# A schedule change in a fused retention + ELU-MLP kernel: attention one unit further ahead, late ELU pass, hand-made plan for units 4 to 11

## Chip, cores, metric

One core of a Trainium2 chip. The metric is the device time of a run in microseconds (us), the median of several runs. "Span" is the time from the first to the last instruction in one profiled run. The "granted clock" is the share of TensorE's full clock that its throttle let through.

## The reference

```python
def _attn_ref(q, k, v):                     # each [8 batches, 8 heads, 576, 64]
    scores = (1 / np.sqrt(64)) * np.matmul(q, k.transpose(0, 1, 3, 2))
    gamma = 1.0 - 2.0 ** (-5.0 - np.arange(H))
    Dmat = np.where(rel >= 0, gamma[:, None, None] ** rel, 0.0)
    return np.matmul(scores * Dmat, v)

def _moe_ref(x, w_in, w_out):               # x [4608, 512], w_in [512, 2048], w_out [2048, 512]
    h = x @ w_in
    g = np.where(h > 0.0, h, np.exp(np.minimum(h, 0.0)) - 1.0)
    return g @ w_out
```

The kernel cuts the 4608 tokens into 36 units of 128 (unit 0 to 35). The units form ten groups: group 0 is units 0 to 3, group 1 is 4 and 5, group 2 is 6 and 7, groups 3 to 9 have four units each. FFN1 of a group needs the attention output `xt` of all its units.

## The kernel before

Names used below. `rqk`, `rv`: a unit's raw q, k, v. `qkn`, `vn`: their bf16 forms. `tr`: transposes in PSUM, copied to `qkT`. `sc`: scores. `pt`: masked scores. `o`: attention product. `ph`: FFN1 output in PSUM, three banks plus one lent by `pm`. `e`, `m`, `g`: the ELU chain on ScalarE (ACT), GpSimd (POOL) and VectorE (DVE). A "slot" is one FFN1 tile or a quarter of an FFN2 row block: four matmuls of 512 columns, or eight of 256.

```python
ps_h = ctx.enter_context(tc.tile_pool(name="ps_h", bufs=3, space=PSUM))   # ph
ps_m = ...bufs=1   # pm          ps_s = ...bufs=1   # sc
ps_o = ...bufs=1   # o           ps_st = ...bufs=1  # st

def turn(u, bank=None):                     # transposes of unit u
    ...
    if u < PE_TURNED:                       # 12
        pool, tag = bank or (ps_o, "o")
        ps = pool.tile([P, 2, HP, P], BF16, name="tr", tag=tag)
        ... 8 TensorE transposes ...
        nc.vector.tensor_copy(t[:, 0], ps[:, 0]); nc.scalar.copy(t[:, 1], ps[:, 1])
    else:
        nc.sync.dma_start_transpose(...)    # by DMA

def stretch(u, ahead=True):
    if ahead: scores(u + 1)
    inter(u); state(u); intra(u)            # the product, into o
    if ahead: masks(u + 1)                  # pt
    put_x(u); state_out(u)                  # xt

def ffn1(g, ft, bank=None):
    ... matmuls into ph ...
    nc.scalar.activation(e, ph, AF.Exp)
    nc.gpsimd.tensor_scalar(m, e, -1.0, 1.0, ALU.add, ALU.mult)
    nc.vector.scalar_tensor_tensor(gt_, ph, 0.0, m, ALU.max, ALU.min)     # g, at once

def prep(u, *engs):                         # casts q and k, scales v; u >= 12: turn by DMA
    ...

for ft in range(NFT):                       # FFN1 of group 0
    ffn1(0, ft, ...)
    if ft == 5:
        load(4, nc.vector)                  # a 1-element memset on VectorE holds the loads back
        for u in range(5, 12): load(u)
for u in range(4): ffn2_half(u, 0)          # needs w_out pieces 0 and 1
prep(4, A, V)
ffn2_half(0, 1)                             # needs w_out pieces 2 and 3
turn(4)
... units 4 to 11 between ffn2_half, FFN1 of groups 1 and 2, FFN2 of group 1 (cut) ...
for g in range(2, NG + 1):                  # FFN1 of g and FFN2 of g - 1 in turns
    ...
    at[-1] -= 3                             # last unit of group g + 1: three slots before the end
```

## Time and profile before

| | before |
|---|---|
| median, 4 runs | 346.38 us (344.27 to 346.76) |
| span of the profiled run | 344.1 us, granted clock 0.994 |
| TensorE busy | 313.9 us |
| start of FFN1 of group 0, transposes of unit 4, FFN1 of group 3, FFN1 of group 4 | 22.7, 47.7, 106.4, 133.0 us |

The last row cuts the run into stages, each read from the timeline of TensorE. The prediction below shows the lines of the profile.

### The profile page before, as it was taken

The page shows a single profiled execution, that of the slowest core. Times are in us where ns is not written, and L with a number is a line of the kernel's source. Part 1 is how long each engine was busy: PE and PEld are TensorE (multiplying, and loading weights), DVE is VectorE, ACT ScalarE, POOL GpSimd, SP SyncE. Part 2 cuts the span into 40 slices and gives each one's busy share as a digit, 9 for nine tenths or more (in the row PEclk, how much of TensorE's full clock was granted, in tenths as well). Part 3 has the DMA queues.
Part 4 walks back from the last instruction along what each step waited for, and adds up shares of the span by engine and source line. Part 5 has one row for each costly group of instructions (what it writes and reads, how often), then busy time and mean ns, then how long its engine had stood idle before and what let it go on. Part 6 is the DMA issues. An engine that isn't in the chain of part 4 may idle for free.

```text
span 344.1 us, 7077 instructions
## 1 busy us (share of the span) xinstructions
PE 313.9 (91%) x2797; PEld 163.0 (47%) x2797; DVE 193.8 (56%) x290; ACT 134.1 (39%) x241; POOL 137.2 (40%) x205
## 2 busy tenths in 40 slices
PE   8889988669488999999899989989998999999995
PEld 3544676555354544445344535444444444444442
DVE  3637534575746787666566746684667465444400
ACT  6436322453233543434344334333343443344411
POOL 3587312353423554444344534443444423233300
PEclk9999999999989999999999999999999999999999
DMA  9999999995069689679857777769878120000021
GB/s 171 198 156 201 184 262 240 225 209 90 4 156 209 150 165 231 134 149 192 179 135 168 158 154 153 154 150 158 168 171 155 60 65 32 30 32 30 30 92 62
DMA packets 149922, 48.70 MB, mean 142 GB/s; under 512 B 138625, under 2 KB 145793, under 8 KB 149889
## 3 DMA queue, kind: packets, MB, share of 16 engines
q1 hardware_dynamic: 141888, 41.96, 59.6%
q0 software_dynamic: 6272, 4.19, 8.5%
q10 hardware_dynamic: 1728, 2.10, 1.9%
q8 instruction: 22, 0.36, 0.5%
q14 instruction: 12, 0.09, 0.1%
HBM read 36.70 MB, written 9.44 MB: 134 GB/s over the span
## 4 chain that ended last, share of the span: by engine, by line
issue 31%; PE 22%; POOL 20%; DVE 12%; SPq 6%; DMA 6%; ACT 1%; POOLq 0%; DVEq 0%; ACTq 0%
POOL m L314 13%; PE pm L329 12%; PE ph L307 9%; SPq L85 6%; POOL vn L177 5%; DVE pt L215 4%; DVE qkn L168 3%; DMA rv<-in_v_dram 3%; DVE g L316 3%; DMA rqk<-in_k_dram 3%; DVE xt L279 2%; POOL w_out_sb L100 1%; POOL w_in_sb L95 1%; PE sc L206 0%; PE o L266 0%
## 5 line engine op out<-in xcount | busy, mean ns | idle before, releaser
L316 DVE SCALAR_TENSOR_TENSOR g<-ph,m 128x512 bf16<-128x512 f32 x144 | 98.4, 688 | 106.6 <-POOL m L314 106.6
L314 POOL TENSOR_SCALAR m<-e 128x512 bf16<-128x512 f32 x144 | 89.6, 624 | 164.1 <-ACT e L312 161.6
L307 PE MATMUL ph<-xt,w_in_sb 128*128 128x512 bf16 (+1 forms) x640 | 145.4, 359 | 6.2 <-DVE xt L279 5.9
L312 ACT ACTIVATE e<-ph 128x512 f32<-128x512 f32 x144 | 85.9, 597 | 141.1 <-PE ph L307 138.9
L329 PE MATMUL pm<-w_out_sb,g 128*128 128x512 bf16 x512 | 129.7, 381 | 1.4 <-DVE g L316 0.7
L307 PEld LDWEIGHTS <-w_in_sb 128*128 128x128 bf16 x640 | 60.3, 98 | 68.1 <-issue 9.2
L329 PEld LDWEIGHTS <-g 128*128 128x128 bf16 x512 | 49.7, 98 | 60.3 <-issue 2.4
L215 DVE TENSOR_TENSOR pt<-sc,mask 128x1024 bf16<-128x1024 f32 x36 | 43.7, 1214 | 6.1 <-PE sc L206 6.0
L177 POOL TENSOR_TENSOR vn<-rv,gk 128x512 bf16<-128x512 f32 x36 | 38.1, 1059 | 17.7 <-DMA rv<-in_v_dram 17.7
L279 DVE TENSOR_TENSOR xt<-o,gx 128x512 bf16<-128x512 f32 x36 | 24.4, 678 | 1.1 <-PE o L266 1.1
L168 DVE CAST qkn<-rqk 128x1024 bf16<-128x1024 f32 x26 | 24.2, 932 | 0.0
L339 ACT COPY ot<-pm 128x512 f32<-128x512 f32 x31 | 18.1, 585 | 15.4 <-PE pm L329 15.4
L206 PE MATMUL sc<-qkT 64*64 64x128 bf16 x576 | 15.0, 222 | 4.4 <-ACT qkT L192 2.7
L206 PEld LDWEIGHTS <-qkT 64*64 64x64 bf16 x576 | 9.4, 106 | 18.8 <-issue 10.3
L266 PE MATMUL o<-pt,vn 128*64 128x128 bf16 x288 | 14.5, 222 | 2.4 <-DVE pt L215 2.4
L190 PE MATMUL tr<-ident,qkn 128*128 128x128 bf16 x96 | 7.9, 226 | 9.6 <-DVE xt L279 7.8
L258 ACT CAST sb<-st 128x256 bf16<-128x256 f32 x32 | 11.9, 372 | 10.7 <-PE st L249 7.7
L192 ACT COPY qkT<-tr 128x512 bf16<-128x512 bf16 x12 | 7.0, 585 | 22.7 <-DVE qkT L191 22.7
L348 PE MATMUL pmh<-w_out_sb,g 128*128 128x256 bf16 x128 | 15.0, 273 | 0.6 <-DVE g L316 0.5
L362 PE MATMUL dum<-warm 128*128 128x512 bf16 x45 | 13.8, 440 | 1.3 <-DVE warm L108 1.3
L348 PEld LDWEIGHTS <-g 128*128 128x128 bf16 x128 | 12.3, 98 | 2.7 <-DVE g L316 0.8
L232 PE MATMUL o<-qkT,sb 64*64 64x128 bf16 (+1 forms) x256 | 12.3, 214 | 0.4 <-DVE xt L279 0.4
(43 smaller groups left out, 84.1 us busy)
## 6 DMA issues: line engine op xcount, KB each, us to landing
rqk<-in_q_dram SPq DMA_DIRECT2D x32, 256.0 KB, 4.1
rqk<-in_k_dram SPq DMA_DIRECT2D x32, 256.0 KB, 4.8
rv<-in_v_dram SPq DMA_DIRECT2D x32, 256.0 KB, 5.0
out_dram<-ot SPq DMA_DIRECT2D x28, 256.0 KB, 2.0
w_in_sb<-in_moe_w_in_dram POOLq DMA_DIRECT2D x4, 512.0 KB, 7.1
w_out_sb<-in_moe_w_out_dram POOLq DMA_DIRECT2D x4, 512.0 KB, 16.0
rqk<-in_q_dram SPq DMA_DIRECT2D x8, 128.0 KB, 4.4
rqk<-in_k_dram SPq DMA_DIRECT2D x8, 128.0 KB, 4.4
```

The costliest lines, as they stand in the source:

```text
L85: nc.sync.dma_start(dst, src[b, :, s0 : s0 + n, :].rearrange("h p d -> p h d"))
L168: engs[0](n, src)
L177: nc.gpsimd.tensor_tensor(n, rv, gk[:, u % R].unsqueeze(2).to_broadcast([P, H, D]), ALU.mult)
L206: nc.tensor.matmul(sc[j * 64 : (j + 1) * 64, i, hp], t[r, 1, hp, j * 64 : (j + 1) * 64], t[r, 0, hp], start=(hp == 0), stop=(hp == HP - 1) ...
L215: nc.vector.tensor_tensor(pt.rearrange("p i h t -> p (i h) t"), scs[u].rearrange("p i h t -> p (i h) t"), m.unsqueeze(1).to_broadcast([P, ...
L279: nc.vector.tensor_tensor(xts[g][:, :, i * P : (i + 1) * P], os_[u], gx[:, :, s0 : s0 + P], ALU.mult)
L307: nc.tensor.matmul(ph[:, i * n : (i + 1) * n], w_in_sb[:, j, f : f + P], xts[g][:, j, :n], start=(j == 0), stop=(j == KJ - 1), skip_group_ ...
L312: nc.scalar.activation(e, ph, AF.Exp)
L314: nc.gpsimd.tensor_scalar(m, e, -1.0, 1.0, ALU.add, ALU.mult)
L316: nc.vector.scalar_tensor_tensor(gt_, ph, 0.0, m, ALU.max, ALU.min)
L329: nc.tensor.matmul(pm, gts[g, ft][:, it * P : (it + 1) * P], w_out_sb[:, ft], start=(ft == 0), stop=(ft == NFT - 1))
L348: nc.tensor.matmul(pm, gts[g, ft][:, it * P : (it + 1) * P], w_out_sb[:, ft, c * 256 : c * 256 + 256], start=(ft == 0), stop=(ft == NFT - 1),)
```

## The change

Its intent is to keep TensorE busy from unit 4 on: no transposes behind `xt`, no FFN1 that waits for the last unit of its group, and no cast, `pt` or `xt` behind a `g` that still waits for its `m`.

```diff
-            pool, tag = bank or (ps_o, "o")
+            pool, tag = bank or (ps_s, "sc")
...
+    def finish(n=0):
+        while late and late[0][0] <= slot[0] - n:
+            _, gt_, ph, m, _ = late.pop(0)
+            nc.vector.scalar_tensor_tensor(gt_, ph, 0.0, m, ALU.max, ALU.min)
+    def tick():                             # called at the end of each ffn1 and ffn2
+        slot[0] += 1
+        finish(3)
...                                         # in ffn1
-        nc.vector.scalar_tensor_tensor(gt_, ph, 0.0, m, ALU.max, ALU.min)
+        late.append((slot[0], gt_, ph, m, (g, ft)))
...                                         # unit 2 of the start
-                G(seen, raws[3][0][0:1, 0, 0, 0:1])      # waits for Q of unit 3
+                G(seen, raws[3][0][0:1, 1, 0, 0:1])      # waits for K of unit 3
                 load_w_in(0)
+                load_w_in(1)
...
-    prep(4, A, V)
+    prep(4, A, G)                           # K cast on POOL, for units 4 to 11
...
+    plan = [(1, 1, n) for n in range(8)] + [(2, 1, n) for n in range(3)]
+    for n in range(5):
+        plan += [(1, 2, n), (2, 1, n + 3)]
+    plan += [(1, 2, n) for n in range(5, 8)]
+    at = {6: (1, 4), 7: (6, 8), 8: (10, 12), 9: (14, 16), 10: (18, 19), 11: (21, 23)}
+    for n, (what, g, s) in enumerate(plan):
+        (f1 if what == 1 else ffn2)(g, s)
+        for u, (a, b) in at.items():
+            if n == a:
+                scores(u); masks(u)
+                prep(u + 1, A, G) if u < 11 else None
+            if n == b:
+                product(u)
+                if u < 11: turn(u + 1)
+                if u > 8: prep(u + 3, V)
+                load_next()
+    scores(12); masks(12)
...                                         # groups 3 and later
-        at[-1] -= 3
+            if n in (4, 9, 13, 18, 23) if g == 3 else n % 8 == 7:
+                ... prep, load_next, stretch of the next unit: five units in group 3's stage
```

More of the change, by code (lines that the diff above doesn't have):

```diff
@@ L297 @@
     gts = {}
+    slot = [0]
+    late = []
+    def finish(n=0):
[5 more added lines that the diff above has]
+        finish(3)
     def ffn1(g, ft, bank=None):
@@ L315, in ffn1 @@
         gt_ = gpool.tile([P, 512], BF16, name="g", tag="g")
-        nc.vector.scalar_tensor_tensor(gt_, ph, 0.0, m, ALU.max, ALU.min)
+        late.append((slot[0], gt_, ph, m, (g, ft)))
         for i in range(512 // n):
             gts[g, ft + i] = gt_[:, i * n : (i + 1) * n]
+        tick()
     acc = {}
@@ L323, in ffn2 @@
         it, part = divmod(s, 4)
+        if late and (g, part * 4 + 3) >= late[0][4]:
+            finish()
         if part == 0:
@@ L331, in ffn2 @@
             )
+        tick()
         if part == 3:
@@ L377, in load_next, with product @@
             nload[0] += 1
+    def product(u):
+        inter(u)
+        state(u)
+        intra(u)
+        put_x(u)
+        state_out(u)
     seen = const.tile([1, 1], FP32, name="seen")
@@ L389 @@
         inter(u)
-        state(u)
-        masks(u)
         if u < 3:
+            state(u)
+            masks(u)
             if u == 2:
-                G(seen, raws[3][0][0:1, 0, 0, 0:1])
+                G(seen, raws[3][0][0:1, 1, 0, 0:1])
                 load_w_in(0)
+                load_w_in(1)
             cast(u + 1, A, A if u == 2 else G)
@@ L400 @@
         else:
+            masks(u)
             dummy(4)
+            state(u)
         intra(u)
@@ L405 @@
         dummy(2)
-    for n in range(1, 4):
+    for n in range(2, 4):
         load_w_in(n)
@@ L415 @@
                 load(u)
+    finish()
     for u in range(4):
         ffn2_half(u, 0)
-    prep(4, A, V)
+    prep(4, A, G)
     ffn2_half(0, 1)
     turn(4)
-    prep(5, A, V)
     ffn2_half(1, 1)
+    prep(5, A, G)
     scores(4)
-    inter(4)
-    state(4)
     masks(4)
     ffn2_half(2, 1)
-    intra(4)
-    put_x(4)
-    state_out(4)
+    product(4)
     turn(5)
@@ L433 @@
     scores(5)
-    prep(6, A, V)
-    inter(5)
-    state(5)
     masks(5)
-    dummy(4)
-    intra(5)
-    put_x(5)
-    state_out(5)
+    prep(6, A, G)
+    dummy(5)
+    product(5)
     turn(6)
-    for i in range(8):
-        ffn1(1, 2 * i, (ps_m, "pm") if i % 4 == 3 else None)
-        if i == 0:
-            prep(7, A, V)
-            scores(6)
-            masks(6)
-        if i == 1:
-            inter(6)
-            state(6)
-            intra(6)
-            put_x(6)
-            state_out(6)
-        if i == 2:
-            turn(7)
-        if i == 4:
-            scores(7)
-            masks(7)
-            prep(8, A, V)
-        if i == 6:
-            stretch(7, ahead=False)
-            prep(9, A, V)
-            load_next()
@@ L465, with f1 @@
-    turn(8)
-    for g in range(2, NG + 1):
-        f1 = [(0, g, s) for s in range(0, NFT, 4 // len(GROUPS[g]))] if g < NG else []
-        f2 = [(1, g - 1, s) for s in range(4 * len(GROUPS[g - 1]))]
-        tot = len(f1) + len(f2)
-        seq = []
+    def f1(g, n):
+        ffn1(g, 2 * n, (ps_m, "pm") if g == 1 and n == 3 else None)
+    plan = [(1, 1, n) for n in range(8)] + [(2, 1, n) for n in range(3)]
+    for n in range(5):
+        plan += [(1, 2, n), (2, 1, n + 3)]
+    plan += [(1, 2, n) for n in range(5, 8)]
@@ new lines @@
+    at = {6: (1, 4), 7: (6, 8), 8: (10, 12), 9: (14, 16), 10: (18, 19), 11: (21, 23)}
[3 more added lines that the diff above has]
+            if n == a:
+                scores(u)
+                masks(u)
+                prep(u + 1, A, G) if u < 11 else None
+            if n == b:
+                product(u)
+                if u < 11:
+                    turn(u + 1)
+                if u > 8:
+                    prep(u + 3, V)
+                load_next()
@@ L472 @@
+    scores(12)
+    masks(12)
+    nxt = [12]
+    for g in range(3, NG + 1):
+        f1s = [(ffn1, g, s) for s in range(NFT)] if g < NG else []
+        f2s = [(ffn2, g - 1, s) for s in range(4 * len(GROUPS[g - 1]))]
+        tot = len(f1s) + len(f2s)
         a = b = 0
         for n in range(tot):
-            if b * len(f1) < a * len(f2) and b < len(f2) or a >= len(f1):
-                seq.append(f2[b])
+            if b * len(f1s) < a * len(f2s) and b < len(f2s) or a >= len(f1s):
+                f, gg, s = f2s[b]
@@ L476 @@
                 b += 1
             else:
-                seq.append(f1[a])
+                f, gg, s = f1s[a]
                 a += 1
-        if g == 2:
-            seq = f2[:2] + [x for ab in zip(f1, f2[2:] + [None, None]) for x in ab if x]
-        nxt = list(GROUPS[g + 1]) if g + 1 < NG else []
-        at = [n for n, (what, gg, s) in enumerate(seq) if what and s % 4 == 3]
-        if g == 3:
-            at = [len(seq) * (i + 1) // 4 - 1 for i in range(4)]
-        at[-1] -= 3
-        if g == 2:
-            at = [5, 9, 12, 14]
@@ L489 @@
-        for n, (what, gg, s) in enumerate(seq):
-            (ffn2 if what else ffn1)(gg, s)
-            if g == 2 and n == 1:
-                scores(8)
-                masks(8)
-            if g == 2 and n in (3, 7, 10):
-                turn(nxt[0] + 1)
-            if nxt and n in at:
-                u = nxt.pop(0)
-                prep(u + 2, V) if u < 10 else None
-                if u >= 9:
+            f(gg, s)
+            if n in (4, 9, 13, 18, 23) if g == 3 else n % 8 == 7:
+                u = nxt[0]
+                if u < NU:
@@ L500 @@
                     prep(u + 3, V)
-                load_next()
-                stretch(u)
-        assert not nxt
+                    load_next()
+                    stretch(u)
+                    nxt[0] += 1
 _INS = ['q', 'k', 'v', 'moe_w_in', 'moe_w_out']
```

## The prediction

> **What bounds the kernel now.** I read first the page's busy times and slices, then a table of windows cut at the stage borders, then the waits of TensorE and its timeline around them.
>
> ```profile
> PE 313.9 (91%) x2797; PEld 163.0 (47%) x2797; DVE 193.8 (56%) x290; ACT 134.1 (39%) x241; POOL 137.2 (40%) x205
> ...
> PE   8889988669488999999899989989998999999995
> ...
> PEclk9999999999989999999999999999999999999999
> DMA  9999999995069689679857777769878120000021
> ```
>
> TensorE is the fullest engine and the slices show where it is not full: slices 6 to 12, some 50 to 110 us. The windows say it in us (columns: length, then busy time and count of each engine, granted clock, DMA share, GB/s):
>
> ```profile
> 22.66:47.74 25.08, 23.20 (x144) 13.90 (x144) 12.51 (x21) 10.92 (x19) 13.35 (x20) 1.00 1.32 206
> 47.74:106.36 58.62, 43.81 (x596) 31.35 (x597) 35.79 (x51) 20.58 (x40) 20.82 (x26) 0.97 0.80 164
> 106.36:132.78 26.42, 25.77 (x256) 12.55 (x256) 19.82 (x27) 11.51 (x21) 13.77 (x20) 1.00 0.90 176
> ...
> 265.90:297.50 31.60, 31.59 (x263) 15.18 (x263) 17.45 (x24) 12.16 (x22) 10.26 (x16) 1.00 0.17 48
> ```
>
> Window 47.74 to 106.36 is the attention of units 4 to 11 with the small groups 1 and 2: TensorE stands still 14.8 of 58.6 us there, no other engine is full, so it is a chain of dependences. The window 265.90 to 297.50 is the model of an undisturbed stage: 32 slots of four 512-column matmuls and four attention units in 31.6 us without idle time. From its timeline a slot is 0.864 us, so a unit costs (31.6 - 32 x 0.864) / 4, close to 1.0 us; between two slots elsewhere I read 1.14 us (8.05 us from unit to unit less 8 slots), and take that.
>
> TensorE's waits (waiter, releaser: total us, times, longest):
>
> ```profile
> PE tr L190 <- DVE xt L279: 7.8, 5, 3.5
> PE ph L307 <- DVE xt L279: 5.9, 7, 1.2
> PE sc L206 <- ACT qkT L192: 2.7, 6, 0.9
> PE o L266 <- DVE pt L215: 2.4, 2, 1.6
> ```
>
> The first is one PSUM bank: the transposes of unit u+1 are written into the bank of `o`, which is free only after `xt` of unit u. The second is the start of a group: its first FFN1 matmul needs `xt` of its last unit, made only three slots before. The timeline has both:
>
> ```profile
> 94.75 1.01 PE L190 MATMUL tr<-ident,qkn 128*128 128x128 bf16 x8 [3.54 <-DVE xt L279]
> 95.56 1.91 PE L329 MATMUL pm<-w_out_sb,g 128*128 128x512 bf16 x4
> ...
> 199.29 1.02 PE L307 MATMUL ph<-xt,w_in_sb 128*128 128x512 bf16 x4 [1.00 <-DVE xt L279]
> ```
>
> After 3.54 us of standing still, four matmuls take 1.91 us instead of 1.03: a table of 94.60 to 98.00 gives a granted clock of 0.51.
>
> **What the Trainium skill says.** "TensorE: Matmul & The Clock Gate", Part 1, says an idle window of about 3.4 us halves TensorE's clock. The trace agrees: 3.54 us idle, then 0.51 for 3.4 us, worth some 1.7 us. "PSUM — Partial Sum Buffer", section "Engine vs sequencer instructions", says the queues of ScalarE, VectorE and GpSimdE are strictly first in, first out. The trace fits: in each stretch `g` waits for POOL's `m` (106.6 us over the run) while a cast, `pt` and `xt` stand behind it on VectorE. "Perfetto Trace Analysis", section "Optimization Strategy", takes repeated gaps on the engine that should be full as a possible sign of too few buffers; here it is one bank with two owners.
>
> **The change part by part.** No arithmetic is added but one dummy matmul (0.22 us).
>
> (a) Start. The first `w_in` load waits for K of unit 3, not Q, so K and V of unit 3 no longer share the DMA engines with it. K landed at 17.4 us where the 1.2 us pace of its forerunners would give 16.2; unit 3 moves about 1 us earlier and FFN1 of group 0 starts near 21.8 instead of 22.66. But `ffn2_half` waits for the last `w_out` pieces (landed 36.8 and 45.7 us), and the unit loads now begin two `g` earlier (the one-element memset stands behind 4 of them, not 6) and take some of their bandwidth. I keep 0.4 us: the transposes of unit 4 at 47.3 instead of 47.74.
>
> (b) Units 4 to 11. Own work of TensorE from 47.74 to 106.36: 128 matmuls of 256 columns by 0.109 us, 32 of 512 by 0.216, 48 halves by 0.109, 8 units by about 1.6 us (transposes 0.45 included), dummies 0.9: 13.9 + 6.9 + 5.2 + 12.8 + 0.9 = 39.7 us. So 18.9 of 58.6 us are loss: 14.8 idle, 1.7 of halved clock, the rest the refilling after each wait. The new plan puts the transposes into the bank of `sc` (free as soon as `pt` is made, which the matmuls before need anyway), sets two to four slots between the scores of a unit and its product, moves the K casts from VectorE (0.43 us) to POOL (0.60 us), and lets cast, `pt` and `xt` pass the `g` that still waits. I walked through the plan slot by slot with the durations of the page (slot 0.87, `pt` 1.21, `xt` 0.68, copies 0.42 and 0.58, `g` 0.69, 1.45 us from a slot's last matmul to its `m`). What still waits: `xt` of unit 5 before the first FFN1 0.4, a `ph` bank held by a late `g` 0.55 and 0.2, `pt` of unit 10 0.1, `g` and `xt` of unit 11 at the end 1.5. That is 2.75 + 39.95 = 42.7 us. The units' data come in time: in the trace V of unit 5 is there at 50.7, of unit 8 at 62.5, of unit 12 at 77.9; my walk wants them at 56, 69 and 81. Stage ends at 90 instead of 106.4: -16.3 us with (a).
>
> (c) Group 3's stage, 24 slots. It now carries five units, not four: 24 x 0.864 + 5 x 1.14 = 26.4 us. VectorE has there 16 x 0.69 + 5 x (0.92 + 1.21 + 0.68) = 25.1 us, nearly full, and late `g` keep `ph` banks, of which there are three. My walk gives waits of 1.0, 0.3, 0.3 and 0.25 us, 1.9 in all: 28.3 instead of 26.4, +1.9.
>
> (d) The later groups. A unit has moved forward from the last stretch: -1.1. The last unit of a group is done eight slots before the group needs it, so the four starts at 166, 199, 232 and 266 us lose their waits: 1.16 + 1.16 + 1.38 + 1.26 = 5.0 us by the matmuls' starts. The 0.8 us before the last FFN2 (output copy of the one `pm` bank) and the 18.9 us from 325.2 on stay.
>
> Sum of the span: 344.1 - 16.3 + 1.9 - 1.1 - 5.0 = 322.6 us. The median time is 2.6 above the profiled span: 325.2. A walk by hand finds too few waits, mostly those of ACT, which also issues output DMAs and must queue; I add 1.3 us for two or three unseen ones: **326.5 us**, 5.8% less.
>
> **Rivals.** (R1) Loads bound units 4 to 8. For it: the DMA row stands at 9 until 77 us and unit 4's K was waited for at 47.7. Against: of TensorE's waits after 48 us none names a load, and loads start earlier now. If they did bind, units 5 to 7 would each wait about 2 us: 332. (R2) VectorE becomes the bound, with late `g` holding `ph` banks. For it: 25.1 of 26.4 us in group 3's stage. Against: the stretches after it have 16 x 0.69 + 4 x 2.81 = 22.3 us in 32.2. If it bit from unit 8 on and in group 3's stage, some 5 us come back: 331. (R3) POOL: the K casts with `vn` (1.04) and `m` in one queue, so that `m` comes 1.6 us late and `g` after it. POOL has 9.9 of 13.7 us in the tightest part by my walk; worth 1 to 4 us. (R4) Nothing gained in (b), because each wait removed hands on to the next link (`qkT` over VectorE, then ACT, 1.0 us in series). Then only (d) stays: about 341. I see no chain of that length with two slots of matmuls between the links.
>
> **Range and chances.** (d) is nearly certain as it is only an order; (b) is two thirds of the gain and rests on a plan without measured waits. Half of (b) lost gives 334; all of the walk right and no unseen wait, with the start's full 0.8 us, 323. So 321.5 to 334, and over 2% faster (under 339.8) with 0.94, within 2% 0.05, slower 0.01.
>
> **What would show it.** Right: no wait of the transposes for `xt`; no slice with a clock under full after the start; the first FFN1 of group 3 near 90 us; the matmuls of the later groups run on over the group starts; PE idle near 14 us where it was 30. (c) shows as waits of FFN1 for `g` of one us and less between 90 and 119 us, with VectorE over 0.9 busy. Wrong: waits for loads of q, k or v after 48 us (R1), `ph` waiting for `g` in the later groups (R2), or POOL `m` waiting behind `vn` with TensorE idle (R3).

## The result

The changed kernel takes 329.47 us (median of 4 runs, 327.83 to 330.89) against 346.38. The ratio is 0.9515, with a 95% interval of 0.9462 to 0.9569. Every ratio here was worked out from the runs of both kernels in the same rounds, so it is not quite the quotient of the quoted medians.

The page of the kernel after, busy tenths in 40 slices, then the granted clock:

```profile
PE   8899979999979999999999999999999999999995
...
PEclk9999998999999999999999999999999999999999
```

Slices are counted from 0. The dips of slices 6 to 12 are gone but for slice 11; slice 5 (41 to 49 us) is lower than before, 7 for 8. The slice with the lowered clock has moved from 95 us to 49 us.

The waits of TensorE in the kernel after (waiter, releaser: total us, times, longest):

```profile
PE pmh L365 <- DMA w_out_sb<-in_moe_w_out_dram: 2.5, 2, 2.1
PE ph L320 <- DVE g L306: 1.6, 2, 1.3
PE sc L206 <- ACT qkT L192: 1.5, 4, 0.7
PE dum L379 <- DVE warm L108: 1.3, 1, 1.3
PE ph L320 <- DVE xt L279: 0.9, 3, 0.4
PE pm L345 <- ACT ot L356: 0.7, 1, 0.7
PE tr L190 <- ACT qkn L171: 0.6, 1, 0.6
```

No transpose waits for `xt` any more (7.8 us before), and FFN1 waits 0.9 us for `xt` instead of 5.9. The largest wait is a new one: `ffn2_half` waits for a piece of `w_out`. Where it falls, the late transposes of unit 4 behind it, and the wait of FFN1 for `g` in group 3's stage:

```profile
47.09 1.59 PE L365 MATMUL pmh<-w_out_sb,g 128*128 128x256 bf16 x8 [2.11 <-DMA w_out_sb<-in_moe_w_out_dram]
...
49.27 1.04 PE L190 MATMUL tr<-ident,qkn 128*128 128x128 bf16 x8 [0.59 <-ACT qkn L171]
...
95.99 1.90 PE L320 MATMUL ph<-xt,w_in_sb 128*128 128x512 bf16 x8 [1.25 <-DVE g L306]
```

The stages of the kernel after, as windows (length, busy time and count of PE, PEld, DVE, ACT, POOL, clock, DMA share, GB/s):

```profile
21.92:49.27 27.35, 23.92 (x145) 14.09 (x145) 12.06 (x20) 10.92 (x19) 14.24 (x22) 0.97 1.27 205
49.27:92.85 43.58, 42.71 (x597) 30.69 (x598) 28.61 (x42) 21.97 (x42) 22.87 (x33) 0.98 1.07 217
92.85:121.04 28.19, 26.84 (x297) 13.13 (x296) 23.76 (x33) 12.29 (x23) 15.21 (x21) 1.00 1.17 217
121.04:152.91 31.87, 31.87 (x277) 15.30 (x273) 20.89 (x30) 13.02 (x24) 15.16 (x22) 1.00 0.96 178
```

The table sets the stages of the spans side by side, with the prediction's working:

| stage | before | predicted | after |
|---|---|---|---|
| start to FFN1 of group 0 | 22.7 | 21.8 | 21.9 |
| to the transposes of unit 4 | 25.1 | 25.5 | 27.4 |
| units 4 to 11, to FFN1 of group 3 | 58.6 | 42.7 | 43.6 |
| group 3 (four units before, five after) | 26.6 | 28.3 | 28.2 |
| groups 4 to 9 and the end | 211.1 | 205.0 | 205.0 |

(Predicted for the last row: 211.1 less 5.0 and 1.1.) The later stages are as predicted to a tenth. What was lost against the sum lies between 22 and 51 us: 1.9 us late at the transposes of unit 4, then a rest of the halved clock in the next stage.

The profiled run was the fastest one, at a clock of 0.995. The other three ran at 0.989 to 0.990 and took 1.3 to 3.1 us longer. Experiment e11 below caught such a run.

### The profile page after: what moved, and what is told of

Read it like the earlier page. It is cut to its first block, busy times and chain, and to the rows that moved or that the text cites. A ratio compares the mean times of both kernels' runs of the same rounds, so it can differ in the third digit from the quotient of the medians.

```text
span 326.0 us, 7097 instructions
## 1 busy us (share of the span) xinstructions
PE 312.9 (96%) x2798; PEld 162.4 (50%) x2798; DVE 186.3 (57%) x282; ACT 135.7 (42%) x243; POOL 142.9 (44%) x213
## 4 chain that ended last, share of the span: by engine, by line
PE 81%; SPq 6%; DMA 6%; DVE 3%; POOL 2%; issue 1%; ACT 1%; ACTq 0%; DVEq 0%
PE ph L320 34%; PE pm L345 33%; SPq L85 6%; DMA rqk<-in_q_dram 4%; PE sc L206 3%; PE o L266 2%; PE o L232 2%; PE st L249 2%; DMA rv<-in_v_dram 2%; PE pmh L365 2%; PE tr L190 1%; DVE g L306 1%; DVE pt L215 1%; POOL w_out_sb L100 1%; POOL w_in_sb L95 0%
## 5 line engine op out<-in xcount | busy, mean ns | idle before, releaser
L279 DVE TENSOR_TENSOR xt<-o,gx 128x512 bf16<-128x512 f32 x36 | 24.6, 684 | 5.5 <-PE o L266 5.5
L365 PE MATMUL pmh<-w_out_sb,g 128*128 128x256 bf16 x128 | 16.0, 282 | 2.5 <-DMA w_out_sb<-in_moe_w_out_dram 2.5
L168 DVE CAST qkn<-rqk 128x1024 bf16<-128x1024 f32 x24 | 18.0, 750 | 0.0
L171 POOL CAST qkn<-rqk 128x512 bf16<-128x512 f32 x10 | 6.1, 611 | 10.8 <-DMA rqk<-in_k_dram 10.8
```

The lines of the kernel that those rows point to most:

```text
L279: nc.vector.tensor_tensor(xts[g][:, :, i * P : (i + 1) * P], os_[u], gx[:, :, s0 : s0 + P], ALU.mult)
L365: nc.tensor.matmul(pm, gts[g, ft][:, it * P : (it + 1) * P], w_out_sb[:, ft, c * 256 : c * 256 + 256], start=(ft == 0), stop=(ft == NFT - 1),)
```

## The experiments

Twelve kernels ran, and all gave correct results. "Against before" is the ratio defined above; "against the changed kernel" is the quotient of two such ratios. The 95% intervals of the ratios are 0.2 to 0.5% wide to each side, so a difference of 0.6% or less between two variants is at their limit and is read together with the stages. One of the six runs of e9 was slow and is left out.

### Even spacing alone, and the front alone

e6: the kernel before with only the new loop of groups 3 and later, `g` at once.

```diff
-    for g in range(2, NG + 1):
+    for g in range(2, 3):                  # old loop, then:
+    nxt = [12]
+    for g in range(3, NG + 1): ...         # loop of the changed kernel
```

> The kernel before with only the loop of groups 3 and later taken from the changed kernel: units at even spacing, one unit further ahead; no late g, old plan for units 4 to 11. Theory (each part of the change is worth what its own stage shows): the waits of FFN1 for xt at the starts of groups 5 to 8 go (5.0 us by the matmuls' starts), nothing else moves but one unit from the last stretch into group 3's stage, where I expect up to 1 us of new waits: span 339 to 340.5 instead of 344.1, ratio about 0.987. Rival (even spacing needs the late g, because in group 3's stage VectorE is full with five units): the stage gets 3 to 5 us longer and the ratio is 0.995 to 1.00.

e7: the reverse. The changed kernel up to unit 11, then the old loop with `g` at once.

```diff
+    finish(); at_once[0] = True            # g in ffn1 at once from here
-    nxt = [12]; for g in range(3, NG + 1): ...
+    for g in range(3, NG + 1): ...         # loop of the kernel before
```

> The changed kernel up to unit 11, then the old loop of groups 3 and later with g at once. Theory: group 3's first FFN1 near 92.9 us as in the changed kernel (106.4 before), the four waits at the starts of groups 5 to 8 of 1.0 to 1.2 us are back, span 330 to 331, ratio about 0.961. With the first experiment the two savings add up to the whole within 1 us. Rival (the parts need each other): the group 3 stage begins with other leftovers, so the sum misses the whole by over 2 us.

e6 measured 0.9837 against before, span 338.3 us. The windows of groups 3, 4 and 5 in e6:

```profile
106.90:133.30 26.40, 25.82 (x291) 13.24 (x295) 20.49 (x28) 12.22 (x23) 13.51 (x20) 1.00 1.03 195
133.30:165.20 31.90, 31.69 (x273) 15.31 (x274) 21.27 (x29) 13.04 (x24) 15.19 (x22) 1.00 0.94 190
165.20:197.30 32.10, 31.89 (x286) 15.57 (x288) 20.92 (x29) 13.36 (x25) 13.89 (x21) 1.00 0.78 164
```

The later stages take 31.9 and 32.1 us, as in the changed kernel, against 33.0 and 33.3 before. The four waits at the group starts are gone. Five units in group 3's stage take no longer than four did before (26.6 us): 26.4 us, the plain sum of slots and units. The rival for e6 falls.

e7 measured 0.969, span 332.4 us. Its stage of units 4 to 11 took 43.2 us, and the later stages were back at 33.0 and 33.3 us:

```profile
50.14:93.30 43.16, 41.79 (x592) 30.13 (x598) 28.56 (x42) 21.85 (x42) 22.99 (x33) 1.00 1.08 220
93.30:121.40 28.10, 25.64 (x252) 12.52 (x257) 22.99 (x31) 11.50 (x21) 14.37 (x20) 1.00 0.96 187
121.40:154.40 33.00, 31.70 (x268) 15.26 (x272) 21.61 (x30) 13.61 (x24) 14.52 (x21) 1.00 0.81 168
```

The expected 330 to 331 us was missed by 1.4 us. FFN1 of group 3 began 0.4 us later than expected (93.3 instead of 92.9 us); the larger part lies in group 3's stage, which took 28.1 us instead of the 26.6 of the kernel before, although it has four units and `g` at once. FFN1 waits 1.25 us for `g` at its entry there, as in the changed kernel. So that wait does not need late `g` in the stage, nor a fifth unit. By ratios the two halves save 1.6% and 3.1%, 4.7% in all; the whole saves 4.85%. They add up.

### What inside the front does it

e8: one word changed in the kernel before, `bank or (ps_o, "o")` to `bank or (ps_s, "sc")`.

> The kernel before with one word changed: the transposes of units 4 to 11 go to the bank of sc instead of o. Theory: the waits of tr for xt (7.8 us idle, five times) go, with the 3.54 us one the halved clock (1.7 us); part is handed on to the next link, qkT for the scores or pt for the product: span 337 to 340, ratio 0.98 to 0.988. Rival (each wait hands on whole, because the old plan leaves too few matmuls between the links): span 343 or more.

It measured 0.9959 (0.9916 to 1.0003), span 341.7 us: some 1.4 us, and by the interval anything from nothing to 2.9. The waits moved on to the next link, `pt`:

```profile
PE tr L190 <- DVE pt L215: 4.4, 2, 3.3
PE o L266 <- DVE pt L215: 2.8, 2, 2.0
```

The wait of `tr` for `xt` is gone, but one of 3.3 us for `pt` has its place, still with the halved clock behind it (at 93 us). The rival was nearer than my theory.

e2: the reverse edit in the changed kernel, `ps_s` back to `ps_o`, with the new plan kept.

> The changed kernel with the transposes of units 5 to 11 back in the bank of o, all else the same. Theory: turn follows put_x directly in the plan, so each transpose waits for xt of the unit just before it, about 0.8 us (0.68 for xt and its start) seven or eight times, and the copies of qkT start later, which the slots behind hide: span 331 to 333 against 326.0. Rival (the order of the plan does it, not the bank): under 1 us more.

It measured 0.9659, 1.5% slower than the changed kernel, span 332.8 us. Its stage of units 4 to 11 took 49.2 us instead of 43.6, and the wait came back seven times:

```profile
PE tr L190 <- DVE xt L279: 5.5, 7, 0.8
```

So the same word is worth some 1.4 us by the ratio in the old order and 5.0 us by the ratio in the new one (5.6 in the stage). The bank and the plan need each other.

e1: the changed kernel with `finish()` straight after `late.append(...)`.

> The changed kernel with g emitted at once, as before, all else the same. Theory: in the stretches the cast, pt and xt stand behind a g that waits for m again, but two to four slots of matmuls hide most of it; where xt starts a group's FFN1 or pt is needed by the product, 0.3 to 0.7 us each come back: span 327 to 329 against 326.0, ratio to the changed kernel 1.003 to 1.009. Rival A (late g is what makes the plan run): over 4 us more, chiefly waits of the products for pt between 60 and 92 us. Rival B (late g only holds ph banks): the 1.25 us wait of FFN1 for g in group 3's stage goes and the span is about 325.

It measured 0.9577, 0.65% slower than the changed kernel (the intervals just overlap), which seemed to fit my theory. The stages say otherwise. Units 4 to 11 took 49.1 us instead of 43.6, with these waits:

```profile
PE o L266 <- DVE pt L215: 3.5, 4, 1.2
PE sc L206 <- ACT qkT L192: 2.3, 5, 0.9
```

The timeline of VectorE in e1 shows one cause: `g` has waited 1.85 us for `m`, `pt` starts only behind it, and the product of that unit starts at 83.19 us instead of 82.7.

```profile
81.32 0.69 DVE L306 SCALAR_TENSOR_TENSOR g<-ph,m 128x512 bf16<-128x512 f32 x1 [1.85 <-POOL m L327]
81.92 1.22 DVE L215 TENSOR_TENSOR pt<-sc,mask 128x1024 bf16<-128x1024 f32 x1
```

Against that loss of 5.5 us in the stage there was a gain I had not thought of. With `g` at once the memset that releases the unit loads stands behind six `g` again, not four, and the stretch from FFN1 of group 0 to the transposes of unit 4 took 25.8 us instead of 27.4. The kernel that differs from e1 only in late `g`, with the loads behind six `g` as well, is e4 below. Against e4, e1 is 1.3% slower, 4.2 us by the ratios. (Its span is 5.6 us longer, but the profile caught e1's slowest run and e4's fastest.) Its stage of units 4 to 11 is 6.3 us longer. So rival A holds: late `g` makes the plan run, and my estimate (1 to 3 us) was too low.

e3: the K casts of units 4 to 11 back on VectorE, `prep(u, A, G)` to `prep(u, A, V)`.

> The changed kernel with the K casts of units 4 to 11 back on VectorE, 0.43 us each instead of 0.61 on POOL. Theory: VectorE has room between 50 and 92 us, so the span stays within 1 us (325.5 to 327). Rival (the casts on VectorE stand in front of pt and xt, and their reads of SBUF hold up POOL): waits for pt come up and the span grows by 2 us or more.

It measured 0.9552, 0.4% slower than the changed kernel, which the intervals alone would not show. Its stage of units 4 to 11 lasted 45.8 us at a clock of 0.96. Less the half of the slow time (1.8 us) that is 44.0, against 42.7 for the changed kernel worked out in the same way (43.6 at 0.98). In this stage FFN1 waits once for `g`, 1.13 us at 67.8 us; the changed kernel has no such wait there. On VectorE a K cast of 1.14 us (the one before it took 0.42) stands in front of that `g`. By this estimate from one profile each, moving the casts is worth some 1.3 us. Whether the cast's place in the queue or its length costs it was not separated.

### The new wait for `w_out`

The changed kernel waits 2.1 us for the last piece of `w_out`, which landed at 47.05 us instead of 45.68. The unit loads began at 27.7 us instead of 30.6, because the memset that holds them back is emitted at a fixed place in the code and now stands behind four `g` on VectorE's queue. The Trainium skill, "DMA: Bandwidth & Descriptors", section "Issuing engines are not separate DMA queues", says that DMAs issued by different engines run on the same 16 DMA engines and interleave. The traces fit: from its issue to its landing the last piece took 21.5 us before and 23.5 after. The two experiments move nothing but the memset.

e4: `if ft == 5` to `if ft == 7` (behind six `g`, as in the kernel before).

> The changed kernel with the unit loads started behind 6 g, as in the kernel before, not 4. Theory (the loads that start earlier delay the last piece of w_out, which landed at 47.05 us instead of 45.68, and TensorE waits 2.1 us for it): w_out lands near 46, the wait of ffn2_half for it falls to 1.2 us or less, transposes of unit 4 at 48.3 to 48.8 instead of 49.27; span 324.5 to 325.5, and less of the halved clock. Rival (the DMA engines are full anyway, and unit 4's data come later by as much): the transposes wait for their casts instead and the span stays at 326.

e5: `if ft == 5` to `if ft == 11` (behind ten `g`).

> As the last, the loads started behind 10 g (some 3.5 us later still). Theory: w_out lands at 43 to 44, no wait of ffn2_half for it, no halved clock at 47 us; unit 4's data now come at 47 to 48.5 and the transposes wait for them up to 1.5 us; units 5 and 6 have enough slack: span 323.5 to 325. Rival (loads bind after all): transposes of units 4 and 5 wait over 2 us, the span is 327 or more.

e4 measured 0.9457, e5 0.9347: 0.6% and 1.8% faster than the changed kernel. In e4 the wait for `w_out` fell to 1.2 us. Part of that is chance: FFN1 began 1.1 us later in this run, and `w_out` landed at 46.9 us, hardly earlier than in the changed kernel. In e5 the wait is gone, the clock is full throughout, and TensorE reads:

```profile
39.23 7.27 PE L365 MATMUL pmh<-w_out_sb,g 128*128 128x256 bf16 x65 [0.54 <-DVE g L306]
47.06 0.62 PE L190 MATMUL tr<-ident,qkn 128*128 128x128 bf16 x8 [0.56 <-ACT qkn L171]
```

`w_out` landed at 45.0 us, unit 4's last data at 47.0 us. Nothing later waits for a load, and the stage of units 4 to 11 takes what the prediction worked out, 42.85 us for 42.7:

```profile
47.06:89.91 42.85, 41.99 (x598) 30.14 (x598) 28.61 (x42) 21.94 (x42) 24.08 (x34) 1.00 1.10 226
```

Since the start varies, it is safer to count from FFN1 of group 0 to the transposes of unit 4, over all fourteen profiles: 26.9 to 27.4 us with the memset behind four `g` (five profiles), 25.1 to 26.0 behind six (five), 23.9 to 24.6 behind ten (four). The last `w_out` piece took 23.5 to 24.3, 21.4 to 22.6 and 18.9 to 20.8 us from issue to landing. The groups do not overlap.

So the loads did not have to start early. The later they started, the faster `w_out` came. Started earlier, they cost the wait and, in four of the five profiles behind four `g`, a halved clock behind it. (In e7 a wait of 2.0 us left the clock full.) e4's rival (unit 4's data late by as much, span still 326) falls.

The wait for `w_out` is not the only path, though. In the changed kernel the transposes wait another 0.59 us for the Q cast of unit 4 on ScalarE, which stands behind the issue of an output DMA:

```profile
48.21 0.34 ACTq L371 DMA_DIRECT2D out_dram<-oth  x1
48.59 0.62 ACT L171 CAST qkn<-rqk 128x512 bf16<-128x512 f32 x1 [3.98 <-DMA rqk<-in_q_dram]
```

The output block was ready at 44.6 us and unit 4's Q had landed at 41.7; the issue came 0.1 us after Q of unit 5 landed (48.1). In e4 it came at 47.7, in e5 at 46.0. So an earlier `w_out` alone would not have brought these transposes forward. The place of the memset moves both paths; how much each is worth, and whether the output DMA really waits for that load, was not tested.

e11: the changed kernel once more, unaltered.

> The changed kernel once more, unaltered, for a second profile beside the next two. Its first profile was its fastest run (326.0 us span, FFN1 of group 0 from 21.9 us); all variants of it since began FFN1 at 22.9 to 23.1 us, waiting for the first piece of w_in. Theory: that wait is usual, and the first profile was the lucky one: FFN1 from 22.9 to 23.1, ffn2_half waits 2 us for w_out, a halved clock behind it, span 327.5 to 329, ratio near 0.951. Rival (the variants changed the start): FFN1 from 21.9 again and span 326.

It measured 0.9516 again (329.95 us). This profile shows the common, slower form: span 327.7 us at a clock of 0.989. The wait for `w_out` is the same, the transposes wait 1.28 us for their cast, and the clock stays halved for two windows, from 47.7 to 54.5 us:

```profile
46.89 1.10 PE L365 MATMUL pmh<-w_out_sb,g 128*128 128x256 bf16 x8 [2.06 <-DMA w_out_sb<-in_moe_w_out_dram]
49.26 1.03 PE L190 MATMUL tr<-ident,qkn 128*128 128x128 bf16 x8 [1.28 <-ACT qkn L171]
50.09 3.62 PE L365 MATMUL pmh<-w_out_sb,g 128*128 128x256 bf16 x16
```

Sixteen half-width matmuls take 3.62 us there and 1.92 us at full clock. The half of my expectation about the start was wrong: FFN1 began at 22.0 us, not 22.9. Of the eight profiles with this start (the changed kernel, e11, e1, e2, e3, e4, e5, e7) two began near 22.0 and six between 22.9 and 23.2, these six waiting about 1 us for the first piece of `w_in`. In all six K of unit 3 had landed at 17.1 to 17.3 us, in the changed kernel and e11 at 16.0 and 16.1. The first `w_in` load now waits for that K.

### A better version

e9: e5, the start's loads as in the kernel before, and at the end of unit 11 the held-back `g` and `pt` of unit 12 ahead of the cast of unit 14. The last is meant for the wait of FFN1 for `g` at 95.99 us, where two `g` stood behind that cast and `pt`.

```diff
-        if ft == 5:
+        if ft == 11:
...
-                G(seen, raws[3][0][0:1, 1, 0, 0:1]); load_w_in(0); load_w_in(1)
+                G(seen, raws[3][0][0:1, 0, 0, 0:1]); load_w_in(0)
...
-                if u > 8: prep(u + 3, V)
+                if u in (9, 10): prep(u + 3, V)
                 load_next()
+    finish()
     scores(12); masks(12)
+    prep(14, V)
```

> The kernel with the loads behind 10 g, and two more edits that show in different stages: the first w_in load waits for Q of unit 3 and the second is issued late, both as in the kernel before; and at the end of unit 11 the g still held back and pt of unit 12 go ahead of the cast of unit 14. Theory: FFN1 of group 0 starts at 22.1 to 22.6 instead of 22.9; in group 3's stage the wait of FFN1 for g (1.25 us) goes: 26.8 to 27.3 us instead of 28.2. Span 321 to 322 against 323.1. Rival for the stage (VectorE is simply full there): it stays at 28 or more, with the wait moved to later banks.

e10: e9 with `g` at once from group 3 on.

> As the last, and from group 3 on g is emitted at once, as in the kernel before. Theory (late g is of use only where cast, pt and xt are urgent, up to unit 11; in group 3's stage it holds ph banks longer, 0.3 us a unit): group 3's stage 26.4 to 26.8, later stages unchanged at 31.9 to 32.1. Span 320.5 to 321.5. Rival (late g helps there too): the stage is longer than in the last kernel.

e9 measured 0.9401 and e10 0.9392, both slower than e5. The wait of FFN1 for `g` at 95.99 us did go, but group 3's stage took 30.2 and 28.4 us, with a new wait (in e9 a halved clock of 3.4 us follows it):

```profile
PE sc L206 <- DMA qkT<-qkn: 2.0, 1, 2.0
```

In e9's DMA queue the transposes of unit 14 stand behind the three loads of unit 17, which my edit had put before them:

```profile
93.64 1.09 SPq L85 DMA_DIRECT2D rqk<-in_q_dram  x1
94.78 1.05 SPq L85 DMA_DIRECT2D rqk<-in_k_dram  x1
95.92 0.89 SPq L85 DMA_DIRECT2D rv<-in_v_dram  x1
96.98 3.30 SPq L194 DMA_TRANSPOSE qkT<-qkn  x2
```

e12: the load of unit 17 after the transposes again.

```diff
-                load_next()
+                if u < 11: load_next()
...
     prep(14, V)
+    load_next()
```

> The combined kernel (loads behind 10 g, first w_in load behind Q of unit 3, held-back g and pt of unit 12 ahead of the cast of unit 14), with the load of unit 17 issued after the transpose of unit 14 again, as in the changed kernel; in the combined kernel it stood before it, and the scores of unit 14 waited 2.0 us for the transpose. Theory (that order on the DMA queue, not the later cast, made the wait): no such wait, group 3's stage 26.4 to 27.2 us instead of 28.2, span 320.5 to 321.8, ratio near 0.929, the fastest of all. Rival (the later cast delays the transpose just as much): the wait stays near 2 us and the span is 322.5 or more.

It measured 323.19 us (322.68 to 323.33), 0.9328 against before, with a full clock in all five runs. Group 3's stage:

```profile
89.40:116.10 26.70, 26.60 (x296) 13.15 (x295) 22.98 (x33) 12.25 (x23) 15.07 (x21) 1.00 1.25 216
```

26.7 us instead of 28.2, and no wait for the DMA transposes. This is the fastest kernel, 2.0% faster than the changed one. It leads e5 by 0.2% by ratio and by 2.0 us in span. With separate rounds on different chips, only the gain in the stage is sure, not the exact lead. FFN1 of group 0 began at 22.2 us here, at 21.8 and 22.3 in e9 and e10.

## Why the prediction was right, and where not

The forecast was 326.5 us in a range of 321.5 to 334, faster with 0.94. The measured 329.47 lies in the range, 3 us above the point. Two slips stand in the sum. Its terms, 344.1 - 16.3 + 1.9 - 1.1 - 5.0, give 323.6 us and not 322.6, so the point should have been 327.5. And the 2.6 us from span to median set the span of one run against the median of others: the profiled run of the kernel before took 345.76 us, 1.7 above its span. The 323 given for the best case does not follow from the sum either (325.2 less 0.4 is 324.8).

- **Part (a), the start: the failed term.** I noted that the loads would begin two `g` earlier and "take some of their bandwidth", and still booked a gain of 0.4 us. Measured in the first profile: 1.5 us later than before at the transposes of unit 4 (49.27 against 47.74), and a halved clock around it (0.51 over 47.4 to 50.9 us; 6.8 us long in e11). Against the changed kernel, the memset behind six `g` as before gains 1.8 us by medians (e4), behind ten 5.5 (e5). The move of the first `w_in` load brought its 0.8 us in two profiles of eight only, and its reason does not hold: K of unit 3 landed late (17.1 to 17.4 us) in two of the six profiles with the old order and early (16.1 to 16.2) in the other four, and FFN1 began at 21.8 to 22.7 us in these six.
- **Part (b), units 4 to 11: right in its steps and its total, but the total is partly luck.** 42.7 us forecast, 42.85 measured with a full clock (e5, e4 42.8), 43.6 with the rest of the halved one. The walk had 39.95 us of own work and five waits of 2.75 us. In e5 TensorE is busy for 41.99 of the 42.85 us, and its timeline names only two waits in this stage, both for `xt`: 0.23 us before the first FFN1 and 0.44 at the end. The waits were put too high and the work too low, by some 2 us each. Nor are the parts independent: the bank alone is worth some 1.4 us (e8), without it the plan loses 5 (e2), without late `g` 4 to 6 (e1 against e4), without the POOL casts about 1.3 (e3).
- **Part (c), group 3: right in size, half right in cause.** 28.3 us forecast, 28.2 measured. I laid four waits of 1.0, 0.3, 0.3 and 0.25 on late `g` holding `ph` banks. The first, measured as 1.25, is a matter of order at its entry: e12 takes it away with late `g` kept, and e7 has it with `g` at once. VectorE was busy for 0.84 of the stage, not the 0.9 and more that I named as a sign. The others measured 0.26 and 0.16 by the matmuls' starts. e10 with `g` at once, less its 1.9 us DMA wait, would be 26.5 against 26.7 in e12. Late `g` as such costs no more than a few tenths there.
- **Part (d), the later groups: right.** 6.1 us forecast with the moved unit, 6.1 measured; e6 shows the same stages with the loop alone.
- **Rivals.** R1 named the wrong loads. None of units 5 to 8 made TensorE wait for its data; it was the weights, and ScalarE's queue before the cast of unit 4, that these loads pushed back. R2 was no bound after group 3. R3 did not show: the changed kernel's two waits for `g` (0.35 us at 25.9, 1.25 at 96.0) both lie outside units 4 to 11, where POOL has the casts. R4 is what the bank alone does (e8), and the plan is what prevents it.
- **The allowance.** 1.3 us for unseen waits and 2.6 us between span and median. The profiled run had 1.8 us between. The other three runs took 1.3 to 3.1 us more, at the lower clock that e11 also had; the second halved window that e11 shows would be 1.7 us of it. Their profiles were not kept.
- **The signs.** One sign of being right failed: a slice with a lowered clock was left after the start.

What stays open: why K of unit 3 lands 1.1 us later in some runs, how the DMA engines share between the weight loads and the unit loads, and why the output DMA on ScalarE's queue was issued so late.

## What to carry to other kernels

When instructions are emitted later in program order, look at everything that uses their place as a clock. Here a memset behind "six g" became one behind "four g", and the loads it released earlier cost about 2 us of a gain of 17; behind "ten g" they would have given 5.5 us more. Judge an early prefetch by what it delays: here loads needed at 47 us, started at 28 instead of 34 us, held up one needed at 45. And a change of a buffer alone can be worth little while the order still ties the links together (some 1.4 us), yet be needed for a new order (5 us), so test it both ways.

## What the Trainium skill lacked or had wrong

- "TensorE: Matmul & The Clock Gate", section "Why this matters for your kernels", asks to avoid idle gaps of more than about 3 us. Gaps of 2 us were enough here: the clock fell at 47.41 us after one wait of 2.11 us, with TensorE busy 1.30 of the 3.41 us before. In e9 it fell after a wait of 2.0 us (busy 1.39 of 3.41), in e1 after two of 1.20 and 1.03 us (1.18 of 3.41). The windows did not have to be idle throughout. Nor is a gap of 2 us always enough: in e7 the border between two such windows, counted back from the next change of clock, cut the wait of 2.04 us in two (the second window, from 47.43 us, was busy 1.74 of 3.41), and the clock stayed full. The emptiest window that cost nothing was one of e8, from 72.5 us, busy 1.48.
- The same page calls the window free-running. The runs fit that, since the same gap costs the clock or not by where it falls (e7), and show the size of the spread in a whole kernel: the same code lost one window in one profile (3.4 us at half clock, TensorE busy 2.8 us of it) and two in the other (6.8 us; busy 2.1 us of the first).
- "DMA: Bandwidth & Descriptors", section "Issuing engines are not separate DMA queues", says DMAs of different engines interleave; what that costs one of them in a whole kernel the page does not give. Here the loads of units 4 and on, started 2.9 us earlier, stretched the last `w_out` piece from 21.5 to 23.5 us (issue to landing).
